# Who scales x by the gates: from GpSimd to VectorE and ScalarE, in an attention block with a mixture of experts behind it

## The chip, the cores and the metric

The kernel runs on one core of a Trainium2 chip. The metric is the device time of one execution in microseconds (us), the median of the runs: 721.62 us for the kernel before (three runs, 719.6 to 724.65). A profile of one execution, which took 726.15 us, tells what each engine did. TensorE appears in it as PE (its matmuls) and PEld (its weight loads), VectorE as DVE, ScalarE as ACT, GpSimd as POOL, SyncE as SP; a q behind the name means the engine's sequencer. SP, ACT and POOL can issue DMAs.

## The reference

Two blocks, one behind the other. First causal attention with a sliding window of 64, over 8 batches, 8 heads, 576 positions and a head dimension of 64:

```python
scores = scale * np.matmul(q, k.transpose(0, 1, 3, 2))
mask = (rel >= 0) & (rel < window)          # rel: query position minus key position
attn = softmax(np.where(mask, scores, -1e9))
attn_out = np.matmul(attn, v)
```

Its result, with the heads side by side, is x: 4608 tokens of 512 values. Then a mixture of 8 experts. Each token goes to one expert, and its result is scaled by that expert's share:

```python
logits = x @ w_gate                         # [4608, 8]
expert_idx = argmax(logits); gate_w = softmax(logits)[expert_idx]
h = np.maximum(x_sorted[lo:hi] @ w1[e], 0.0)   # tokens sorted by expert; w1: 512 x 1024
y_sorted[lo:hi] = h @ w2[e]                     # w2: 1024 x 512
out = gate_w[:, None] * y                       # back in the order of the tokens
```

Since the gate is positive, scaling x by it before the expert gives the same result as scaling y behind it. That is what the kernel does.

## The kernel before

**The attention phase** takes the first 218 us or so of the profile. The batches are worked in four *pairs* (`bg` 0 to 3) of two batches. A pair is 9 token tiles of 128 tokens (`NTB`), in three *chunks* of three tiles. A *unit* is a pair and two heads; there are 16 units, and each has three *steps*, one chunk each: 48 steps, `s` = 0 to 47, 12 to a pair. `step(s)` is a pipeline written out by hand, and every engine takes its instructions in the program's order:

- PE makes the scores of chunk s+1 (L628), multiplies the weights of chunk s-1 with v (`weighted`, L674), adds the logits of s-3, transposes the softmax of s (L659), transposes q and k of s+3 (L587, L595), and transposes x of s-2 (L699).
- VectorE masks the scores of s+1 and takes their row maxima (L641), copies one half of the transposed softmax of s out of PSUM (L661), divides s-1 by its row sums and writes it into x (`divided`, L684 to L688), and then does whatever is listed for the step in `todo`.
- ScalarE does the exponentials (L651), the other half's copy (L661) and the copies of the transposes (L600, L702), then its part of `todo`.
- GpSimd copies parts of v so that they lie where a matmul can read them (`load_v`, L567 to L573, issued in each third step, for the unit after next), then its part of `todo`.

`weighted` writes one PSUM bank, `banks[6]`; so its matmuls in step s+1 wait until `divided` in step s has read that bank.

x of a chunk is gathered over a pair's four units in an SBUF tile `xs` of 128 x 3 x 512. The pool has 7 buffers, taken in turn (chunk `3*bg + c`).

**Routing.** In the step behind a pair's last logits, `after` lists what remains of that pair in `todo`, counted in steps n from there (for the pairs 0 to 2, n = 0 is step 15, 27 and 39):

- `choose`: the argmax, the softmax, the gates and each token's rank at its expert, in five parts, all small operations on VectorE.
- `place` (L800): two VectorE operations on 128 x 128 bf16 for a token tile, which feed the table of slots.
- `weigh` (L807): scales one token tile of x (128 x 512, fp32) in place by its gates, one value per partition.
- `store` (L815): writes a chunk of x to DRAM (`x_dram`), as DMAs on the queue of GpSimd. A chunk that spans both batches takes two or three DMAs.

For the first two pairs, `place`, `weigh` and `store` are listed side by side; for the third pair they are packed into n = 2 to 5. Then `first_tiles` (n = 6) makes a first table of slots, for which PE waits (L907 to L914), and gathers the first expert's tokens from `x_dram` on GpSimd's queue. The fourth pair is weighed by ScalarE alone, after the attention phase.

**The expert phase** takes the rest: tiles of 256 tokens, gathered from `x_dram`, multiplied with one expert's w1 and w2, and scattered into the output. Sums of weight blocks (L140) are made on GpSimd. If an expert has more tiles than the unrolled code foresees, `any_number` runs instead; with these inputs it does not.

Of the kernel before, what the change touches and what calls it, by code (L numbers as in the profile page):

```python
# [11 lines left out]
F32 = mybir.dt.float32  # L12
# [3 lines left out]
ALU = mybir.AluOpType  # L16
AX = mybir.AxisListType
# [7 lines left out]
def _ins(ap: bass.AP, axis: int, n: int) -> bass.AP:  # L25

    dims = [list(d) for d in ap.ap]
    dims.insert(axis, [0, n])
    return bass.AP(tensor=ap.tensor, offset=ap.offset, ap=dims)


def _inner(ap: bass.AP, n: int) -> bass.AP:
    return _ins(ap, len(ap.ap), n)
# [3 lines left out]
def kernel(  # L37
# [10 lines left out]
    nc = tc.nc  # L48
    P = nc.NUM_PARTITIONS
    B, H, S, D = q.shape  # L50
    NT, DM = out.shape
    E = moe_w_gate.shape[1]
# [9 lines left out]
    NTB = BG * S // P  # L62
# [5 lines left out]
    NTILE = (NT + TB - 1) // TB + E - 1 + NE  # L68
# [27 lines left out]
    expert_i = consts.tile([P, NTILE], I32, name="expert_i")  # L96
# [4 lines left out]
    V, G = nc.vector, nc.gpsimd  # L101
# [48 lines left out]
    def sums_w1(e):  # L150
        form(left_sums(G, s1s[e % NW], *w1q(e)))

    def sums_w2(e):
        form(right_sums(G, s2s[e % NW], *w2q(e)))

    def load_w1(e):
        return nc.sync.dma_start(out=w1s[e % NW][:], in_=w1v[e])

    def load_w2(e):
        nc.sync.dma_start(out=w2s[e % NW][:], in_=w2v[e])  # L160
# [7 lines left out]
    lane = consts.tile([P, P], BF16, name="lane")  # L168
# [9 lines left out]
    with tc.tile_pool(name="tmp", bufs=1) as tmp:  # L178
# [8 lines left out]
        for i in range(BG):  # L187
# [12 lines left out]
            out=before[:], in_=ones[:], pattern=[[1, P]], compare_op=ALU.is_gt, fill=0.0, base=0,  # L200
# [6 lines left out]
    nt, cum, start, chunk0 = (consts.tile([P, E], F32, name=n) for n in ("nt", "cum", "start", "chunk0"))  # L207
    rt = ctx.enter_context(tc.tile_pool(name="rt", bufs=1))
# [26 lines left out]
    ST = 3  # L235
# [4 lines left out]
    v_m = Memory(consts.tile([P, 3 * 2 * BG * NV * 2 * VW], F32, name="v_m"))  # L240
# [27 lines left out]
    def form_all(parts):  # L268
        for _ in parts:
            pass  # L270

    def gather(tokens):
        G.tensor_copy(out=at_g[:], in_=tokens)
        for c in range(C):
            G.indirect_dma_start(  # L275
                out=xg[c], out_offset=None, in_=x_dram[:, :],
                in_offset=bass.IndirectOffsetOnAxis(ap=at_g[:, c : c + 1], axis=0),
            )
# [31 lines left out]
    def turned_blocks():  # L310

        rows = xg_all.rearrange("p c (g b j) -> p c g b j", b=P // QD, j=QD)
        for a in range(P // QD):
            for b in range(P // QD):
                V.transpose(  # L315
                    out=xn[b * QD : (b + 1) * QD, :, :, a * QD : (a + 1) * QD].rearrange("p c g i -> p (c g) i"),
                    in_=rows[a * QD : (a + 1) * QD, :, :, b, :].rearrange("p c g j -> p (c g) j"),
                )
                yield
# [5 lines left out]
    def keep_turned():  # L325
        for c in range(C):
            nc.scalar.copy(out=xq[:, :, c], in_=xn[:, c])  # L327
# [151 lines left out]
    def body(e, last, after, full, between=None, next_x=True):  # L479

        finish()
        scatter(perm_i[:, last])
        if between is not None:
            between()
        blocks = turned_blocks() if next_x else iter(())
        if not full:
            half_tile(e, blocks, after, next_x)
            return
        form_all(hidden(e, blocks))
        parts = output(e, blocks, next_x)  # L490
        next(parts)
        if after is not None:
            gather(perm_i[:, after])
        form_all(parts)

    with tc.manual_schedule(), ExitStack() as held, ExitStack() as brief:
# [381 lines left out]
        def after(s, routing, bg):  # L878

            do = lambda n, op: todo.setdefault(s + n, []).append(op)  # L880
            part = lambda: next(routing, None)
            if bg < last - 1:
                for n in range(5):
                    do(n, part)

                for m in range(NTB):
                    do(5 + m * 2 // 3, partial(place, bg * NTB + m))
                    do(5 + m * 2 // 3, partial(weigh, bg, m, G))
                    if m % ST == ST - 1:
                        do(5 + m * 2 // 3, partial(store, bg, m // ST, G))  # L890
                return

            for n in (0, 0, 1, 2, 2):
                do(n, part)
            for m in range(NTB):
                do(3 + m // 3, partial(place, bg * NTB + m))
                do((2, 2, 3, 3, 4, 4, 4, 5, 5)[m], partial(weigh, bg, m, nc.scalar if m in (2, 6) else G))
                if m % ST == ST - 1:
                    do(3 + m // ST, partial(store, bg, m // ST, G))
            do(6, first_tiles)  # L900
# [153 lines left out]
    with tc.manual_schedule():  # L1054
        load_w1(1)
        load_w2(1)
        def at(n):
            n = nc.s_assert_within(
                n, 0, NTILE - 1, skip_runtime_bounds_check_because="a tile with a token is one of the NTILE"
            )  # L1060
            return lambda ahead: bass.ds((n + ahead) * C, C)

        def expert(e):

            fulls, tiles, first = regs[e]
            if 0 < e < E - 1:
                load_w1(e + 1)
                load_w2(e + 1)

            def one(n, full, between=None):  # L1070
                slots = at(first + n)
                ends = e == E - 1 and (n == KT - 1 or not full)
                body(e, slots(0), None if ends or e == E - 1 and n == KT - 2 else slots(3), full, between, not ends)

            def more(n, between=None):

                with tc.If(tiles > n) as some_left:  # L1077
                    with tc.If(fulls > n, preferred_fallthrough_block=False) as full:
                        one(n, True, between)
                        if n + 1 < KT:  # L1080
                            more(n + 1)
                    with full.Else():
                        one(n, False, between)
                if between is not None:
                    with some_left.Else():
                        between()

            if e:
                one(0, True, partial(sums_w2, e))
            more(1 if e else NE, partial(sums_w1, e + 1) if e + 1 < E else None)  # L1090

        def any_number():

            tiles_of = rt.tile([P, E, NTILE], F32, name="tiles_of")
            V.tensor_tensor(
                out=tiles_of[:], in0=_inner(cum[:], NTILE), in1=_ins(lane[:, 0:NTILE], 1, E), op=ALU.is_le
            )
            with nc.allow_low_precision("integers"):
                V.tensor_reduce(out=expert_i[:], in_=tiles_of[:].rearrange("p e t -> p t e"), axis=AX.X, op=ALU.add)
            _, (tiles,) = nc.values_load_multi_w_load_instructions(  # L1100
                places_i[0:1, E : E + 1], min_val=0, max_val=NTILE,
                skip_runtime_bounds_check_because="a sum of numbers of tiles, at most NTILE for any tokens",
            )
            with tc.For_i(NE, tiles) as i:
                _, (e,) = nc.values_load_multi_w_load_instructions(
                    expert_i[0:1, bass.ds(i, 1)], engines=(mybir.EngineType.SP,), min_val=0, max_val=E - 1,
                    skip_runtime_bounds_check_because="a tile that is numbered belongs to an expert",
                )
                for w, view in ((w1s[0], w1v), (w2s[0], w2v)):
                    nc.sync.dma_start(out=w[:], in_=view[bass.ds(e, 1)].rearrange("o p n d -> (o p) n d"))  # L1110
                sums_w1(0)
                sums_w2(0)
                slots = at(i)
                gather(perm_i[:, slots(1)])
                form_all(turned_blocks())
                keep_turned()
                sums_x([xn[:, c] for c in range(C)])
                form_all(hidden(0))
                form_all(output(0, iter(()), False))
                finish()  # L1120
                scatter(perm_i[:, slots(1)])

        with tc.If(most < KT + 1) as few:  # L1123
            for e in range(E):
                expert(e)
            finish()
            scatter(perm_i[:, bass.ds(end * C, C)])
        with few.Else():
            finish()
            scatter(perm_i[:, NE * C : (NE + 1) * C])  # L1130
            any_number()
# [28 lines left out]
```

## Time and profile before

| what | us |
|---|---|
| median of the runs (lowest, highest) | 721.62 (719.6, 724.65) |
| the profiled execution, its span | 726.15, 724.4 |
| PE / VectorE / ScalarE / GpSimd busy | 689.7 / 497.8 / 258.5 / 350.7 |
| `weigh` on GpSimd (L813) | 25 x 1.565 = 39.2 |
| `weigh` on ScalarE (L811) | 11 x 0.71 = 7.3, two of them in the third pair |
| `place` on VectorE (L802) | 72 operations, 29.2 |
| `load_v`'s copies on GpSimd (L567, L569, L573) | 45.6 |
| start of VectorE's mask in step 19, 20, 21 | 97.39, 102.56, 106.45 |
| in step 27, 28, 29 | 129.34, 133.94, 137.68 |
| in step 31, 32, 33 | 145.47, 150.04, 154.13 |
| in step 39, 40, 41 | 176.69, 182.13, 185.90 |
| in step 42, 43, 44, 45 | 191.74, 195.70, 200.73, 205.49 |

The page gives the busy time of each engine, its 40 slices, and the costliest groups of instructions by line. The busy share is a mean over phases with different limits, so the steps around the change are read by themselves. A step is told here by the start of VectorE's first mask (L641) in it, which is its first instruction of that step. "Start to start" is the time from the start of one instruction to that of the next on an engine that does not idle; on VectorE it is shorter than the duration shown, since two instructions overlap at their ends.

### The profile page before, as it was taken

How to read it: one execution, taken by the hardware profiler on the slowest of the kernel's cores; microseconds unless marked ns; L12 is line 12 of the kernel's file. 1: busy time of each engine (PE TensorE's matmuls, PEld its weight loads, DVE VectorE, ACT ScalarE, POOL GpSimd, SP SyncE). 2: the span in 40 equal slices, each digit the busy share in tenths (PEclk: the TensorE clock that was granted, in tenths of full speed). 3: DMA queues.
4: the chain of work that ended last, by engine and by line, in shares of the span. 5: the costliest groups of instructions: out<-in, count | busy, mean ns of one | idle time of the engine just before them, and what ended most of it. 6: DMA issues, size and time to landing. Idle time of an engine off the chain costs nothing. (4 is left out here: it accounts for less than half of the span.)

```text
span 724.4 us, 17946 instructions
## 1 busy us (share of the span) xinstructions
PE 689.7 (95%) x6882; PEld 607.1 (84%) x6882; DVE 497.8 (69%) x1636; ACT 258.5 (36%) x653; POOL 350.7 (48%) x360
## 2 busy tenths in 40 slices
PE   5999999999879999999999999999999999999993
PEld 3887788888768898797999999899889799889993
DVE  3575898898965858675866686677766677666731
ACT  4787788888754211111211221112111111111110
POOL 4213748459375025937462356445274745272011
PEclk9999999999999999999999999999999999999997
DMA  8998898789361382715211531440261620111000
GB/s 159 219 195 186 176 188 230 168 188 235 106 194 47 121 291 81 258 59 202 102 38 60 161 133 57 154 170 30 88 243 59 242 69 30 61 37 61 2 30 28
DMA packets 137289, 93.37 MB, mean 129 GB/s; under 512 B 117009, under 2 KB 117009, under 8 KB 137171
## 3 DMA queue, kind: packets, MB, share of 16 engines
q1 hardware_dynamic: 127858, 62.16, 32.5%
q0 software_dynamic: 8736, 27.53, 11.7%
q10 hardware_dynamic: 576, 2.10, 0.9%
q8 instruction: 74, 1.21, 0.7%
q14 instruction: 45, 0.36, 0.2%
HBM read 72.89 MB, written 20.45 MB: 129 GB/s over the span
## 5 line engine op out<-in xcount | busy, mean ns | idle before, releaser
L315 DVE STREAM_TRANSPOSE v_m<-qk_m 32x256 f32<-32x256 f32 x304 | 132.4, 435 | 9.0 <-DMA qk_m<-x_dram,at_g 3.4
L344 PE MATMUL bank<-qk_m,s 128*128 128x128 f32 x1024 | 122.5, 275 | 1.0 <-DVE qk_m L365 1.0
L344 PEld LDWEIGHTS bank<-qk_m,s 128*128 128x128 f32 x1024 | 118.3, 192 | 1.2 <-issue 1.2
L275 POOL DMA_INDIRECT qk_m<-x_dram,at_g x38 | 41.0, 1080 | 142.4 <-DVE v_m L315 114.0
L651 ACT ACTIVATE pr<-pr,mx 128x128 f32<-128x128 f32 x288 | 89.7, 391 | 36.3 <-DVE mx L641 36.3
L344 PE MATMUL bank<-qk_m,w 128*128 128x128 f32 x768 | 93.8, 275 | 1.0 <-PEq L1077 0.9
L344 PEld LDWEIGHTS bank<-qk_m,w 128*128 128x128 f32 x768 | 90.6, 192 | 4.6 <-issue 4.2
L641 DVE CUSTOM_DVE_ANT_0 pr<-bank,mask 128x128 f32<-128x128 f32 x288 | 64.4, 286 | 30.7 <-PE bank L628 28.1
L295 POOL DMA_INDIRECT out_dram<-v_m,at_s x42 | 42.5, 1012 | 87.7 <-DVE v_m L384 85.1
L384 DVE TENSOR_TENSOR v_m<-bank,v_m 128x256 f32<-128x256 f32 (+1 forms) x95 | 43.8, 480 | 45.0 <-PE bank L388 30.1
L569 POOL COPY v_m<-v_m 64x520 f32<-64x520 f32 x32 | 19.8, 619 | 73.1 <-DMA v_m<-in_v_dram 72.5
L140 POOL TENSOR_TENSOR s<-w 128x1024 f32<-128x1024 f32 x22 | 52.2, 2372 | 0.0
L674 PEld LDWEIGHTS bank<-v_m,pT 128*64 128x64 f32 x1152 | 41.3, 141 | 12.0 <-DVE xs L688 5.8
L674 PE MATMUL bank<-v_m,pT 128*64 128x65 f32 x1152 | 47.9, 232 | 2.9 <-DVE xs L688 2.8
L388 PE MATMUL bank<-qkT_m,v_m 128*128 128x256 f32 x216 | 48.3, 379 | 0.0
L351 ACT COPY qk_m<-bank 128x512 f32<-128x512 f32 x16 | 9.4, 587 | 108.8 <-PE bank L344 63.2
L628 PE MATMUL bank<-qkT_m 64*64 64x128 f32 x1152 | 45.9, 290 | 0.1
L388 PEld LDWEIGHTS bank<-qkT_m,v_m 128*128 128x128 f32 x216 | 41.0, 190 | 5.5
L595 PE MATMUL bank<-ident,qk_m 128*128 128x128 f32 x256 | 37.0, 288 | 8.9 <-DMA qk_m<-in_q_dram 7.7
L444 PEld LDWEIGHTS bank<-qk_m,w 128*128 128x128 f32 x320 | 43.9, 190 | 0.9 <-issue 0.7
L444 PE MATMUL bank<-qk_m,w 128*128 128x160 f32 x320 | 44.4, 299 | 0.4 <-ACT qk_m L327 0.4
L659 PE MATMUL bank<-ident,pr 128*128 128x128 f32 x288 | 43.1, 287 | 0.0
(174 smaller groups left out, 1231.1 us busy)
## 6 DMA issues: line engine op xcount, KB each, us to landing
w<-in_moe_w_dram SPq DMA_DIRECT2D x11, 2048.0 KB, 10.0
qk_m<-in_q_dram SPq DMA_DIRECT2D x72, 128.0 KB, 3.8
qk_m<-in_k_dram SPq DMA_DIRECT2D x72, 128.0 KB, 3.7
v_m<-in_v_dram SPq DMA_DIRECT2D x64, 128.0 KB, 3.9
qk_m<-in_moe_w_dram SPq DMA_DIRECT2D x3, 2048.0 KB, 10.4
x_dram<-xs POOLq DMA_DIRECT2D x6, 512.0 KB
x_dram<-xs POOLq DMA_DIRECT2D x3, 768.0 KB
w<-in_moe_w_dram ACTq DMA_DIRECT2D x4, 512.0 KB, 4.3
```

The lines of the kernel that those rows point to most:

```text
L140: op()
L295: put = G.indirect_dma_start(out=out[:, :], out_offset=bass.IndirectOffsetOnAxis(ap=at_s[:, c : c + 1], axis=0), in_=ys[c], in_offset=None ...
L315: V.transpose(out=xn[b * QD : (b + 1) * QD, :, :, a * QD : (a + 1) * QD].rearrange("p c g i -> p (c g) i"), in_=rows[a * QD : (a + 1) * QD ...
L344: nc.tensor.matmul(acc[:, f, :], lhsT=a[:, g, f * P : (f + 1) * P], rhs=b[:, g, :], start=(first and f == 0 and g == 0), stop=(g == HG - 1 ...
L384: plus = lambda out, a, b: V.tensor_tensor(out=out, in0=a, in1=b, op=ALU.add)
L388: nc.tensor.matmul(acc, lhsT=a[:, f, :], rhs=b[:, f, :], start=(start and f == 0), stop=(stop and f == HF - 1), skip_group_check=True,)
L444: nc.tensor.matmul(acc[:, i], lhsT=w1[:, g, f * P : (f + 1) * P], rhs=xq[:, g].rearrange("p c s -> p (c s)")[:, 0:HALF], start=(i + g == 0 ...
L628: nc.tensor.matmul(out_, lhsT=qT[rows, t, a * WINDOW : (a + 1) * WINDOW], rhs=rhs, start=True, stop=True, skip_group_check=True,)
L641: V.tensor_tensor_reduce(out=prs[h][:, m, :], in0=scs[h][:, m, :], in1=mask[:, m0 + m, :], scale=-scale, scalar=-2 * MASKED, op0=ALU.add, ...
L651: nc.scalar.activation(out=y, in_=y, func=AF.Exp, scale=-1.0, bias=mx[:, h, m : m + 1])
L659: nc.tensor.transpose(out=tr[:, m, :], in_=prs[h][:, m, :], identity=ident[:])
L674: nc.tensor.matmul(px[a * D : (a + 1) * D, h, m, :], lhsT=pTs[h][:, m, a * D : (a + 1) * D], rhs=vt[:, h, :], start=True, stop=True, skip_ ...
```

## The change

`weigh` of the first two pairs goes from GpSimd to VectorE, one token tile a step in n = 4 to 12, and `place` is spread in the same way, one tile a step in n = 5 to 13. Before, both stood at n = 5 to 10, in steps of two, one, two, one tiles. The stores stay on GpSimd's queue, each in the step of its chunk's last `weigh`: n = 6, 9 and 12 instead of 6, 8 and 10.

In the third pair the seven `weigh` that GpSimd had are shared out: ScalarE has tiles 0, 1, 3 and 6 (before: 2 and 6), VectorE the other five. They stand at n = 2, 3, 3, 4, 4, 4, 5, 5, 5 instead of 2, 2, 3, 3, 4, 4, 4, 5, 5. Its `place` and `store` stay where they were.

In `any_number`, which is not run here, a table no longer has an SBUF tile of its own but lies in memory that the expert phase uses.

```diff
                 for m in range(NTB):
-                    do(5 + m * 2 // 3, partial(place, bg * NTB + m))
-                    do(5 + m * 2 // 3, partial(weigh, bg, m, G))
+                    do(5 + m, partial(place, bg * NTB + m))
+                    do(4 + m, partial(weigh, bg, m, V))
                     if m % ST == ST - 1:
-                        do(5 + m * 2 // 3, partial(store, bg, m // ST, G))
+                        do(4 + m, partial(store, bg, m // ST, G))
                 return
...
                 do(3 + m // 3, partial(place, bg * NTB + m))
-                do((2, 2, 3, 3, 4, 4, 4, 5, 5)[m], partial(weigh, bg, m, nc.scalar if m in (2, 6) else G))
+                do((2, 3, 3, 4, 4, 4, 5, 5, 5)[m], partial(weigh, bg, m, nc.scalar if m in (0, 1, 3, 6) else V))
                 if m % ST == ST - 1:
                     do(3 + m // ST, partial(store, bg, m // ST, G))
...
-            tiles_of = rt.tile([P, E, NTILE], F32, name="tiles_of")
+            tiles_of = v_m(2080, E, NTILE)
             V.tensor_tensor(
-                out=tiles_of[:], in0=_inner(cum[:], NTILE), in1=_ins(lane[:, 0:NTILE], 1, E), op=ALU.is_le
+                out=tiles_of, in0=_inner(cum[:], NTILE), in1=_ins(lane[:, 0:NTILE], 1, E), op=ALU.is_le
             )
```

More of the change, by code (lines that the diff above doesn't have):

```diff
@@ L1092, in any_number @@
         def any_number():
-            tiles_of = rt.tile([P, E, NTILE], F32, name="tiles_of")
+            tiles_of = v_m(2080, E, NTILE)
             V.tensor_tensor(
-                out=tiles_of[:], in0=_inner(cum[:], NTILE), in1=_ins(lane[:, 0:NTILE], 1, E), op=ALU.is_le
+                out=tiles_of, in0=_inner(cum[:], NTILE), in1=_ins(lane[:, 0:NTILE], 1, E), op=ALU.is_le
             )
             with nc.allow_low_precision("integers"):
-                V.tensor_reduce(out=expert_i[:], in_=tiles_of[:].rearrange("p e t -> p t e"), axis=AX.X, op=ALU.add)
+                V.tensor_reduce(out=expert_i[:], in_=tiles_of.rearrange("p e t -> p t e"), axis=AX.X, op=ALU.add)
             _, (tiles,) = nc.values_load_multi_w_load_instructions(
```

## The prediction, made before the result was known

> **What bounds the kernel now.** I read the page's busy times first, then its 40 slices, then a table of windows (us from the start; busy time of each engine, then the granted clock, DMA share, GB/s), then who waits, then the VectorE, PE and GpSimd timelines.
>
> ```profile
> PE 689.7 (95%) x6882; PEld 607.1 (84%) x6882; DVE 497.8 (69%) x1636; ACT 258.5 (36%) x653; POOL 350.7 (48%) x360
> ...
> POOL 4213748459375025937462356445274745272011
> ```
> ```profile
> 102.50:129.30 26.80, 26.19 (x453) 21.68 (x455) 24.11 (x133) 23.17 (x70) 23.37 (x27) 1.00 0.83 205
> 150.00:173.00 23.00, 22.68 (x397) 18.75 (x393) 21.48 (x116) 20.02 (x60) 19.38 (x27) 1.00 0.91 225
> 173.00:191.70 18.70, 18.17 (x321) 15.17 (x318) 15.68 (x87) 13.61 (x42) 12.46 (x14) 1.00 0.58 159
> 191.70:205.50 13.80, 11.78 (x205) 9.41 (x204) 13.60 (x68) 11.14 (x31) 8.56 (x8) 1.00 0.53 179
> ```
>
> PE is busy for 95% of the span. In the first two windows, where GpSimd weighs the first and the second pair, PE is full (26.19 of 26.80, 22.68 of 23.00) and VectorE is close behind (24.11, 21.48). In the fourth, the third pair's, it is the other way round: VectorE has 13.60 of 13.80 and PE 11.78. GpSimd is not the bound in any. What it weighs, only its own stores wait for:
>
> ```profile
> L813 POOL TENSOR_SCALAR xs<-xs,gate x25: 1554/1565/1632, 103.9 to 205.3; 128x512 f32<-128x512 f32 x25
> ...
> who waited for it (us, times):
>   POOL x_dram L822: 8.7, 3
>   POOL x_dram L829: 0.9, 3
> ```
>
> So 25 x 1.565 = 39.2 us of GpSimd go, and by themselves are worth nothing. The change is paid or repaid on VectorE. PE waits for it in two ways: weighted (L674) for the division L688, which frees its one bank, and once for L907:
>
> ```profile
> PE bank L914 <- DVE hi_e L907: 2.7, 1, 2.7
> PE bank L674 <- DVE xs L688: 2.6, 4, 0.9
> ```
>
> GpSimd does cost VectorE something. The same three pairs of L802, first with GpSimd idle, then beside L813:
>
> ```profile
> 195.26 0.31 DVE L802 TENSOR_SCALAR lo<-lane,low,tok_a 128x128 bf16<-128x128 bf16 x1
> 195.48 0.31 DVE L802 TENSOR_SCALAR lo<-lane,low,tok_b 128x128 bf16<-128x128 bf16 x1
> ```
> ```profile
> 199.16 0.30 DVE L802 TENSOR_SCALAR lo<-lane,low,tok_a 128x128 bf16<-128x128 bf16 x1
> 199.39 0.74 DVE L802 TENSOR_SCALAR lo<-lane,low,tok_b 128x128 bf16<-128x128 bf16 x1
> 199.99 0.30 DVE L802 TENSOR_SCALAR lo<-lane,low,tok_a 128x128 bf16<-128x128 bf16 x1
> ```
>
> Idle, a place (two L802) takes 0.44 from start to start; beside L813, 0.83. That is what the change can win.
>
> **The price of one weigh on VectorE, w.** No row has this operation on VectorE. TENSOR_TENSOR from SBUF takes 0.421 for 256 elements and 0.689 for 512: 0.153 fixed and 1.05 ns per element written, while reading two. If one input of 512 goes by elements read, it is 0.153 + 0.27 = 0.42; if by elements written, 0.69 (L452, TENSOR_SCALAR of 480 from PSUM, has 0.657). Both ends are equally near, so I take the middle, 0.55. Start to start is 0.09 less than a duration (L802: 0.31 against 0.22): w = 0.46, ends 0.33 and 0.60. The Trainium skill, "VectorE: DVE Perf Modes", section on the perf-mode tier table, has fp32 tensor_scalar in SBUF at two elements a cycle (1227 ns for 2048); my estimate from it is 0.42 for 512, which is the low end, and the sum would be +1.3 by it instead of +2.6.
>
> A rule against the change: the Trainium skill, "GPSIMD Engine Reference", section 4.1 Engine selection, calls one-input elementwise work on GpSimd "roughly line-rate", so moving it would win nothing. L813's 1.565 us, 3.06 ns an element, disagrees; the sum does not use it.
>
> **Step by step.** A step of VectorE is mask, copy L661, division: 2.69 us when nothing is waited for (118.15 to 120.84), 3.3 when the copy waits for PE's transposes, then the listed ops. PE's own step is 3.42, 3.96 or 4.18 (steps 4 to 8, with nothing listed on VectorE), 3.83 on average. So the listed ops may take 3.83 - 2.69 = 1.14 before VectorE becomes the bound.
>
> *Steps 21-26 and 33-38* (0.9 in each: a place and a weigh): 2.69 + 0.90 = 3.59 a step, under 3.83. After a short PE step VectorE comes 3.3 + 0.9 - 3.42 = 0.8 late; in steps 21 and 33 it is 1.6 and 1.45 late now and PE has no gap there. Cost 0, hidden behind PE; without that cover, 0.9 a step less the collisions that go.
>
> *Steps 19 and 31* get one weigh each after the routing arithmetic, where VectorE is late already: in the steps behind, L674 starts 0.05 after L688 ended and PE has a gap (0.48 at 104.83, 0.1 at 152.7). A later L688 goes straight through: 0.46 twice. Steps 20 and 32 place one tile instead of two, so the lateness does not pass on. **+0.92** (0.66 to 1.20).
>
> *Steps 27 and 28* get a place and a weigh, and a place, beside the next routing. VectorE's step 28 starts at 134.83 instead of 133.94, 1.4 behind PE's scores; step 29 starts 0.8 late, and 0.8 cost 0.1 in step 32. **+0.3** (0 to 0.9).
>
> *Steps 39 and 40*, the same for the second pair, hit the third pair's routing, which VectorE already bounds (step 39 is 5.45 long, PE waits for L661 at 183.72). Step 39 starts 0.72 late, gets back 0.56 since L661 no longer waits, and has 0.90 more: 183.19 instead of 182.13. The place in step 40 goes into 0.4 idle. **+1.0** (0.9 to 1.2).
>
> *Steps 42-45.* VectorE is never idle from 191.74 to L907 at 208.3, so all counts. Five weighs: 5 x 0.46 = 2.30. Without L813 the six L802 take 1.33 instead of 2.40 (198.33 to 200.73) in step 43 and 2.14 (203.35 to 205.49) in step 44: -1.88. **+0.42** (-0.23 to +1.12). ScalarE's four weighs (0.707 each, two more than now) fall in steps 41 to 44, where it waits for the mask; cost 0, at most 0.7 if that wait went.
>
> *Stores.* GpSimd's queue holds v's copies (L567-L573) too. The store of chunk 1 moves from step 23 to 24 (35 to 36), behind the copies of the v load issued there, which wait for its DMA. That load's last issue ends at 118.78, lands 3.9 later (the page's median), its copies end by 124, the store is issued by 125 (now 121.3), and lands 3.2 to 6.2 later: 131 at worst. Its buffer, one of seven, is written again by L688 in step 27 at 132.07: cost 0, with about 1 us left, and the like in step 39 (179.4). Chunk 2 goes from step 25 to 27, behind copies that wait till 140.4; its buffer is wanted only in step 37. The third pair's last store now lands at 211.7, and the gather behind it waits for perm_e from VectorE until 212.75: a free GpSimd brings nothing there. The moved table tiles_of lies in a branch that is not run: 0.
>
> **Sum**: 0.92 + 0.3 + 1.0 + 0.42 = **+2.6 us** (1.3 to 4.4). After 211 PE is full (497 of 513), so it stays to the end. The profiled execution took 726.15 (span 724.4): 728.8 for it. The runs' median is 721.62, 4.5 below that execution; the same difference gives **724.2**, 0.4% slower. About 1% is what a measurement of this kernel can tell from no change.
>
> **Rivals.**
> 1. *Slower: VectorE becomes the bound in every weighing step.* If a weigh costs the high end and collides with v's copies as L802 does (0.60 + 0.4 = 1.0), the listed ops are 1.44: over 1.14, the point from which it decides (w above 0.70). Steps 21-26 and 33-38 then cost 12 x 0.30 = 3.6, steps 19 and 31 2.0, 27-28 1.4, 39-40 1.5, 42-45 5.0 - 1.88 = 3.1: +11.6, 733. For: L796 took 0.60 instead of 0.17 beside a copy at 101.1. Against: copies fill only 2.9 of some 11.5 us. 0.09.
> 2. *The store of chunk 1 lands late* and L688 waits for it: some 1.5 us twice on top of the forecast, 727. For: the thin margin. Against: the worst landing was assumed. 0.10.
> 3. *Slightly faster.* The low w, and VectorE's added lateness lies under waits that PE has anyway: steps 42-45 give -0.23, the rest nothing, and copies done earlier spare 1 to 2 us of collisions: 720. PE's gaps between 90 and 211 that VectorE causes are 0.48 + 0.29 + 0.24 + 1.42 + 0.48 + 2.71 = 5.6 us; even all of them are 0.8%, which speaks against more. 0.20.
> 4. *The change does not do what it says*: L813 stays in the profile. Nothing points to it. 0.01, 721.6.
>
> **Chances.** Forecast 0.60. Faster by over 1%: 0.04 (only past all of those gaps). Slower by over 1%: rival 1, and a little of 2: 0.11. Within: 0.85. The range takes in rivals 2 and 3 and the spread of the runs (719.6 to 724.65): 718.5 to 729.
>
> **What would show it.** POOL's 39 us at L813 are gone; VectorE has 23 TENSOR_SCALAR xs<-xs,gate of 0.42 to 0.69; L802 is back at 0.31 in steps 43 and 44; no weighing step of 21-26 has a new PE gap; the gap ahead of L914 stays near 2.7 and comes some 2.6 us later than 205.9. Wrong I would be if w is over 0.70, if L688 waits for x_dram, or if PE's gaps shrink.

## The result, and the profile after

The changed kernel takes 724.39 us (median of 13 runs, 723.03 to 728.24) beside 722.33 for the kernel before (13 runs, 719.6 to 724.69). The ratio is 1.0036, with a 95% interval of 1.0020 to 1.0052: 0.4% slower, within what was called no change, but a real loss. The ratio makes it 2.6 us (1.4 to 3.8); the two medians are 2.1 apart. The forecast was 724.2 and +2.6. The size was right; of the terms that made it up, only some were.

From the page of the changed kernel: its span, busy times, instructions and GpSimd's slices (lines left out are marked by dots):

```profile
span 722.7 us, 17947 instructions
...
PE 688.7 (95%) x6882; PEld 606.5 (84%) x6882; DVE 500.7 (69%) x1659; ACT 259.9 (36%) x655; POOL 311.1 (43%) x335
...
POOL 5223734234155025947462356545275745272011
```

GpSimd lost 39.6 us of work. VectorE gained only 2.9, although its 23 weighs add 11.6. Most of the difference came back from its places (L802), which went from 29.2 to 22.7 us, now that GpSimd stretches them less. The weigh and the place on VectorE, by line (durations in ns: least, median, greatest):

```profile
L813 DVE TENSOR_SCALAR xs<-xs,gate x23: 471/479/719, 97.8 to 204.1; 128x512 f32<-128x512 f32 x23
```
```profile
L802 DVE TENSOR_SCALAR lo<-lane,low,tok_a x36: 303/306/632, 100.8 to 251.3; 128x128 bf16<-128x128 bf16 x36
L802 DVE TENSOR_SCALAR lo<-lane,low,tok_b x36: 301/307/659, 101.0 to 251.6; 128x128 bf16<-128x128 bf16 x36
```

A weigh takes 0.479 us, 0.396 from start to start (0.55 and 0.46 were taken, within 0.42 to 0.69). The greatest duration of a place's operation fell from 0.958 to 0.659.

The single profile of the kernel before began its step 19 at 97.39, 3.5 us later than that of the changed kernel (93.91), for reasons that lie ahead of any weighing. So that span (724.4) stands above the span after (722.7), and only stretches behind step 19 can be compared. A second profile of each kernel was taken for that (the runs *before_again* and *after_again* below), with step 19 at 94.30 and 94.37. (All fourteen profiles of this document have it between 93.1 and 98.7.) Each row is a stretch of steps, from the start of VectorE's first mask in the first to that in the step behind the last, in us:

| steps | before, twice | changed, twice | forecast of the difference |
|---|---|---|---|
| 19, 20 | 9.06, 8.10 | 8.11, 8.19 | +0.46 |
| 21-25 | 19.33, 19.33 | 19.19, 18.99 | 0 |
| 26-28 | 11.90, 11.90 | 14.40, 14.23 | +0.3 |
| 29, 30 | 7.79, 7.83 | 7.62, 7.71 | 0 |
| 31, 32 | 8.66, 8.75 | 8.76, 8.58 | +0.46 |
| 33-37 | 18.99, 18.99 | 19.37, 19.20 | 0 |
| 38-41 | 18.62, 18.62 | 19.34, 19.81 | +1.0 |
| 42-44 | 13.74, 13.74 | 13.85, 13.85 | +0.42 |
| 19-44 | 108.10, 107.27 | 110.64, 110.55 | +2.6 |

The whole is +2.5 to +3.4. From step 45 to the end the two kernels are alike: 518.9 and 519.3 us before, 518.1 and 519.3 changed. How far such a stretch varies by itself shows in steps 19 and 20, where five of the profiles ran the schedule of before (7.41 to 9.06 us) and four the changed one (7.81 to 8.40).

The largest part, +2.4 in steps 26 to 28, is where the forecast had 0.3. What happens there is one wait, and PE idles with it. Steps 27 and 28 in the changed kernel, then in the second profile of the kernel before (stretch, its length, busy times of PE, PEld, VectorE, ScalarE and GpSimd, granted clock, DMA share, GB/s):

```profile
125.48:135.60 10.12, 8.14 (x132) 6.46 (x128) 7.84 (x46) 6.59 (x19) 0.29 (x1) 1.00 1.24 208
```
```profile
125.30:133.63 8.33, 8.33 (x146) 7.01 (x148) 6.93 (x39) 6.92 (x20) 5.71 (x7) 1.00 0.81 203
```

VectorE's timeline of the changed kernel in step 27 (start, duration, engine, line, operation; in brackets the idle time before it and who ended it):

```profile
127.21 0.15 DVE L684 TENSOR_SCALAR rec<-bank 128x6 f32<-128x6 f32 x1
127.39 0.19 DVE L685 RECIPROCAL rec<-rec 128x6 f32<-128x6 f32 x1
129.63 0.56 DVE L688 TENSOR_TENSOR xs<-bank,rec 128x384 f32<-128x384 f32 x1 [2.04 <-DMA x_dram<-xs]
130.10 0.31 DVE L802 TENSOR_SCALAR lo<-lane,low,tok_a 128x128 bf16<-128x128 bf16 x1
```

L688 wants to write the next pair's x into the buffer of the first pair's chunk 1, and the store of that chunk has not landed. GpSimd's timeline tells why the store was late:

```profile
114.07 0.29 POOL L567 COPY v_m<-qk_m 64x128 f32<-64x128 f32 x1
121.21 0.62 POOL L569 COPY v_m<-v_m 64x520 f32<-64x520 f32 x1 [6.85 <-DMA v_m<-in_v_dram]
...
123.48 0.51 POOL L573 COPY v_m<-v_m 64x390 f32<-64x390 f32 x1
123.93 1.30 POOL L822 DMA_DIRECT2D x_dram<-xs  x2
```

GpSimd idles for 6.85 us in the copies of a v load, with the store behind them in its queue. The last of its two DMAs is issued by 125.23, and L688 is let go at 129.63. In the second profile of the kernel before, which began step 19 as early, the same store stands ahead of those copies and goes out at 119.54, 4.4 us sooner; L688 in step 27 does not wait:

```profile
119.54 1.36 POOL L822 DMA_DIRECT2D x_dram<-xs  x2
120.94 0.32 POOL L567 COPY v_m<-qk_m 64x128 f32<-64x128 f32 x1
121.30 0.62 POOL L569 COPY v_m<-v_m 64x520 f32<-64x520 f32 x1
```

What PE waited for in the attention phase after the change (total us, times, longest):

```profile
PE bank L674 <- DVE xs L688: 3.5, 6, 1.0
PE bank L699 <- DVE pT L661: 3.2, 3, 1.4
PE bank L914 <- DVE hi_e L907: 2.7, 1, 2.7
```

The waits for L688 grew from 2.6 us in the first profile of the kernel before to 3.5, and the wait for L907 stayed at 2.7, as forecast.

### The profile page after: what moved, and what is told of

The parts are those of the page before. It is cut to its first block, busy times and chain, and to the rows that moved or that the text cites. A ratio compares the mean times of both kernels' runs of the same rounds, so it can differ in the third digit from the quotient of the medians.

```text
span 722.7 us, 17947 instructions
## 1 busy us (share of the span) xinstructions
PE 688.7 (95%) x6882; PEld 606.5 (84%) x6882; DVE 500.7 (69%) x1659; ACT 259.9 (36%) x655; POOL 311.1 (43%) x335
```

## The experiments

Two theories stood against each other. **Theory 1**, the forecast's: VectorE pays for what was added in steps where it is late already. **Theory 2**: the late store. The runs' medians are spread by several us, so an interval on a ratio is some 0.2 to 0.3% to each side; the stretches from the profiles are finer, but each is from one execution, and varies by itself as said above.

**The store ahead of the v load again** (e1_store_ahead). Tile 5 is weighed one step earlier, all else as changed:

```diff
-                    do(4 + m, partial(weigh, bg, m, V))
+                    do((4, 5, 6, 7, 8, 8, 10, 11, 12)[m], partial(weigh, bg, m, V))
                     if m % ST == ST - 1:
-                        do(4 + m, partial(store, bg, m // ST, G))
+                        do((4, 5, 6, 7, 8, 8, 10, 11, 12)[m], partial(store, bg, m // ST, G))
```

> The changed kernel, but tile 5 of the first two pairs is weighed one step earlier, so that the store of chunk 1 stands in step 23 (35) as in the kernel before, ahead of the copies of the v load of step 24 (36). Theory 1 (the price: VectorE's added operations meet steps where it is late already): nothing changes, some 724.4, +2.0 us on the kernel before. Theory 2 (the late store: the division L688 in step 27 waits 2.0 us for the store of chunk 1, whose buffer it writes again): the wait is gone, 722.3 to 722.8, within 0.5 us of the kernel before, and steps 27 and 28 take some 8.4 instead of 10.1 us.

Measured: 724.97 us, ratio 1.0027 (1.0001 to 1.0054). L688 waited for no DMA; steps 27 and 28 took 8.13 us instead of 10.12, and steps 19 to 44 108.87 instead of 110.64 and 110.55. So in the profile the late store was worth 1.7 of the 2.5 to 3.4 us. The medians don't show that gain: 1.7 us off the changed kernel's 1.0036 would make 1.0013, and the interval of e1 holds that and no gain as well. How much of the measured loss the wait makes up over many executions is not shown. Steps 38 to 41 took 19.80, no less than in the changed kernel: that part of theory 1 stands by itself.

**Only the stores late** (e2_late_stores). The kernel before, weighing on GpSimd, with the stores' new steps:

```diff
-                        do(5 + m * 2 // 3, partial(store, bg, m // ST, G))
+                        do(4 + m, partial(store, bg, m // ST, G))
```

> The kernel before, with GpSimd weighing as it did, but the stores of the first two pairs listed where the changed kernel has them (n = 6, 9, 12). Theory 1: VectorE has nothing new, so no difference, 0 us. Theory 2: L688 waits for x_dram in step 27, perhaps also in step 39, for 1 to 2 us each: +1 to +3 us.

Measured: 724.21 us, ratio 1.0016 (0.9990 to 1.0042). The time alone can't tell it from no change. In the profile the wait is there, without one weigh on VectorE; steps 27 and 28 took 9.80 instead of 8.33. VectorE's line of L688 in this kernel's timeline:

```profile
130.24 0.56 DVE L688 TENSOR_TENSOR xs<-bank,rec 128x384 f32<-128x384 f32 x1 [2.15 <-DMA x_dram<-xs]
```

Here the copies ahead of the store did not wait for their DMA (they ran from 119.35 to 122.50); their own length was enough, and the store went out at 122.44. With e1 this settles that the wait comes with the store's place in GpSimd's queue, not with the engine that weighs. It came in step 27 alone; step 39, for which the same was feared, never waited in any profile.

**Each half of the change by itself** (e3_first_two_pairs, e4_third_pair). In e3 the third pair's line of `weigh` is as before; in e4 the three lines of the first two pairs are.

> The change in the first two pairs alone; the third pair as before, with GpSimd weighing seven tiles. From the prediction's terms with the measured 0.40 us a weigh: steps 19 and 31 0.8, 27 and 28 0.3, 39 and 40 0.95: +2.0 us on the kernel before. Theory 2 gives +2 for another reason. If the relief in the third pair is worth more than I worked out, this kernel is slower than the changed one, +3 or more.

> The change in the third pair alone; the first two pairs as before, on GpSimd. The prediction's term for steps 42 to 45 with the measured 0.40 us a weigh: 5 x 0.40 - 1.88 = +0.1 us. A rival, that the collisions of VectorE with GpSimd cost more than those seen in L802: -1 us or less.

Measured: the first two pairs alone 725.45 us, ratio 1.0039 (1.0014 to 1.0064), with L688 waiting 3.17 us; the third pair alone 722.12 us, 0.9996 (0.9971 to 1.0022). No loss is shown outside the first two pairs. Steps 42 to 44, in which VectorE is the bound, took 13.86 us with the third pair's change and 13.77 without it: five weighs on VectorE cost 5 x 0.40 = 2.0 and the end of the collisions gave 1.9 back, as worked out. In e4 L688 waited 1.30 us too, with the old steps of the stores: there three weighs of GpSimd stand ahead of the store, which went out at 122.07 instead of 119.54. The first two pairs of e4 are those of the kernel before, so that kernel is at the edge of this wait itself.

**Nothing weighed in the first two pairs** (e5_no_weigh). The changed kernel with this line taken out; tokens of those pairs go into the experts unscaled:

```diff
-                    do(4 + m, partial(weigh, bg, m, V))
```

> The changed kernel without the weighing of the first two pairs (their tokens go unscaled into the experts); places, stores and the third pair as changed. So the price of the 18 weighs on VectorE is measured by itself. Theory 1 (they are paid in steps 19, 31 and 39, 0.40 us each, and nowhere else): 1.2 us less from step 19 to step 46 than in the changed kernel, and the wait of L688 for x_dram, if that comes with the store's place, stays. Theory 2 (all of the loss is the late store): no less than 116.5 us from step 19 to step 46 (changed kernel 116.9), and L688 waits about 2 us.

Measured: 724.13 us, ratio 1.0028 (1.0009 to 1.0047), still slower than the kernel before, with no weigh at all in the first two pairs. L688 waited 1.78 us for x_dram. Steps 19 to 44 took 108.23, 2.4 less than the changed kernel. Most of it lies in steps 19 and 20 (6.95 against 8.11) and 31 and 32 (7.92 against 8.76), and none in steps 21 to 25 and 33 to 37 (19.60 and 19.60, against 19.19 and 19.37). So the weighs in those ten steps are free, and the others look paid for, by one execution.

**Each weigh twice** (e6_twice), to look for the point from which VectorE decides:

```diff
                 engine.tensor_scalar(out=y, in0=y, scalar1=s, scalar2=None, op0=ALU.mult)
+                if bg < last - 1:
+                    engine.tensor_scalar(out=y, in0=y, scalar1=1.0, scalar2=None, op0=ALU.mult)
```

> The changed kernel with each weigh of the first two pairs done twice on VectorE (the second time by 1.0, same tile): some 0.38 us more in each of the 18 steps. The prediction's threshold says that the listed operations of a step cost nothing up to 1.14 us; here they are 0.44 + 0.40 + 0.38 = 1.22, so 12 x 0.08 = 1.0 us in steps 21 to 26 and 33 to 38, and 0.38 each in steps 19, 27, 31 and 39: +2.5 us on the changed kernel. If VectorE is the bound in all of those steps already, 18 x 0.38 = +6.8. If PE hides it all, 0.

Measured: 731.7 us, ratio 1.0112 (1.0092 to 1.0132): by the two ratios 0.76% or some 5.5 us above the changed kernel, twice what was expected, and most of the 18 x 0.34 = 6.1 us that were added. (Its profile began step 19 at 98.73, and L688 of step 27 came only at 130.86 and did not wait, though the store stood where the changed kernel has it.) Busy times in steps 21 to 25 and 33 to 37, first in the changed kernel, then in this one (stretch, its length, PE, PEld, VectorE, ScalarE, GpSimd, granted clock, DMA share, GB/s):

```profile
102.02:121.20 19.18, 19.15 (x329) 15.88 (x325) 17.79 (x97) 17.05 (x51) 5.91 (x12) 1.00 0.92 209
151.98:171.35 19.37, 19.37 (x343) 16.37 (x340) 17.89 (x97) 17.34 (x51) 7.61 (x15) 1.00 0.87 207
```
```profile
107.81:128.61 20.80, 20.00 (x337) 16.22 (x339) 20.29 (x102) 17.44 (x51) 7.91 (x15) 1.00 0.88 217
159.24:179.27 20.03, 19.75 (x337) 16.20 (x339) 19.52 (x102) 17.44 (x51) 7.95 (x15) 1.00 0.81 206
```

With one weigh a step PE fills the stretch and VectorE has 1.4 us left. With two, VectorE has 0.5 left and PE has gaps of 0.8 and 0.3: the bound is passing over, at 0.44 + 0.40 + 0.34 = 1.18 us listed a step. That agrees with a threshold of 1.14, which lies between 0.84 (free) and 1.18 (not free). The price beyond it was too low: 1.6 and 0.7 us for the two stretches against 0.4 each.

**Another packing** (e7_packed). Places and weighs of the first two pairs in steps 20 to 26 (32 to 38), clear of the routing, stores in steps 21, 23 and 26:

```diff
-                    do(5 + m, partial(place, bg * NTB + m))
-                    do(4 + m, partial(weigh, bg, m, V))
+                    do((5, 6, 7, 8, 9, 9, 10, 11, 11)[m], partial(place, bg * NTB + m))
+                    do((5, 6, 6, 7, 8, 8, 9, 10, 11)[m], partial(weigh, bg, m, V))
                     if m % ST == ST - 1:
-                        do(4 + m, partial(store, bg, m // ST, G))
+                        do((5, 6, 6, 7, 8, 8, 9, 10, 11)[m], partial(store, bg, m // ST, G))
```

> The changed kernel with weighs and places of the first two pairs packed into steps 20 to 26 (32 to 38): none meets the routing in steps 19, 27, 28, 31, 39 and 40, and the stores of chunks 1 and 2 stand in steps 23 and 26, ahead of the next v load. Listed operations a step: 0.84 to 1.28 us. Theory 1: the 0.95 of steps 39 and 40 and the 0.8 of 19 and 31 go, 0.5 comes in the fuller steps. Theory 2: the wait of L688 goes. Both together: within 0.5 us of the kernel before, 722 to 723.2; 38 to 42 takes 18.3 to 18.7 us (changed kernel 19.34) and no wait of L688 for x_dram.

Measured: 724.42 us, ratio 1.0021 (1.0003 to 1.0039). No wait of L688. Steps 38 to 41 took 19.04, less than the changed kernel but above the 18.3 to 18.7 expected: step 38 now has 1.28 listed. Still slower than the kernel before, by the medians: its steps 19 to 44 took 108.30 us, where that kernel's two profiles have 107.27 and 108.10.

**The steps of before, on VectorE** (e8_steps_of_before): places, weighs and stores at `5 + m * 2 // 3`, weighed by V.

> VectorE weighs the first two pairs in the very steps in which GpSimd did it before (places and stores as before, too); third pair as changed. This parts the engine from the move. Steps 20, 22 and 24 (32, 34, 36) then hold two places and two weighs, 1.68 us, the others 0.84, 1.26 on average against the 1.14 that PE hides: 12 x 0.12 = 1.4 us by theory 1, and none of the 0.95 in steps 39 and 40: +1.4 on the kernel before. Theory 2: the store of chunk 1 is earlier than with GpSimd's weighing, so no wait of L688.

Measured: 726.03 us, ratio 1.0037 (1.0022 to 1.0053). No wait of L688, and 18.60 for steps 38 to 41, as before. But steps 21 to 25 took 20.35 and 33 to 37 19.96, 2.0 us together more than before (19.33, 18.99), where 1.4 was expected for these and steps 20 and 32. Two places and two weighs in a step are too much even if the next step has room: its steps 20 to 25 took 4.59, 3.46, 4.65, 3.46, 5.01 and 3.77 us.

**A second profile of each kernel, and two variants.** before_again is the kernel before:

> The kernel before once more, for a second profile. In the first one the steps up to 19 took 97.4 us and L688 in step 27 did not wait; in the four other profiles with the old stores or the late ones and an early start (93.6 to 95.1) it waited 1.3 to 3.2 us. If the wait hangs on how early the attention is, since the loads of v end at about the same time in every execution: with step 19 starting near 94, L688 waits about 1 us here too; with a start near 97, not.

Measured: 722.97 us, ratio 0.9985 (0.9958 to 1.0012). Step 19 began at 94.30 and L688 did not wait: the expectation was wrong. Of the five profiles with the stores in their old steps (both of the kernel before, e4, e8, e9), e4 alone shows the wait.

after_again is the changed kernel:

> The changed kernel once more, beside the other kernels of this call. With step 19 starting near 94: L688 waits 2 us, and 116.5 to 117 us from step 19 to 46. With a start near 97: no wait, and some 115. Time: 1.002 to 1.005 of the kernel before.

Measured: 726.16 us, ratio 1.0038 (1.0016 to 1.0060), the first result once more. L688 waited 2.04 us, to the hundredth as in the first profile.

e10_places_of_before puts the places back (`do(5 + m * 2 // 3, ...)`) and leaves weighs and stores as changed:

> The changed kernel with the places of the first two pairs back in their old steps (20 to 25, 32 to 37); weighs and stores as changed. Theory 1: the place leaves steps 39 and 40 (27 and 28), so steps 38 to 41 take 0.4 to 0.8 us less than the changed kernel's 19.3; steps 20, 22, 24 have 1.28 listed, 0.1 above what PE hides. Theory 2: the wait of L688 in step 27 stays, 2 us with an early start. 0.3 to 0.8 us less than the changed kernel in all.

Measured: 725.48 us, ratio 1.0032 (1.0009 to 1.0055). L688 waited 2.10 us. Steps 38 to 41 took 18.65, which is the 18.62 of before: with the places of steps 38 to 40 gone, the weighs of steps 38 and 39 alone cost nothing there. But with the places and no weighs (e5) they took 19.03, also less than the changed kernel's 19.34 and 19.81: it takes both to make the +0.7 to +1.2. Steps 19 and 20 took 8.83 instead of 8.11 and 21 to 25 19.88 instead of 19.19, so most of it was lost again, if these single executions hold.

e9_mixed leaves the first two pairs on GpSimd, but for tile 5, and has the third pair as changed:

```diff
-                    do(5 + m * 2 // 3, partial(weigh, bg, m, G))
+                    do(5 + m * 2 // 3, partial(weigh, bg, m, V if m == 5 else G))
```

> Third pair as changed; the first two pairs as before, on GpSimd, but for tile 5, which VectorE weighs in step 23 (35), so that the store of chunk 1 has one weigh of 1.57 us less ahead of it on GpSimd. Listed operations in step 23: 0.84, under 1.14, so free by theory 1; the wait of L688 (1.3 us with the first two pairs as before and an early start) goes by theory 2: 0.997 to 1.000 of the kernel before, and 113 us or less from step 19 to 46 without the throttle's part. If neither holds, 1.000 or above.

Measured: 722.63 us, ratio 0.9992 (0.9963 to 1.0021). No wait of L688, and 107.32 us for steps 19 to 44, which is no less than the better profile of the kernel before (107.27). It can't be told from the kernel before, and nothing that was run is shown to beat it.

## Why the prediction was right, and where it was wrong

**GpSimd's 39.2 us are worth nothing by themselves: right, as far as the runs show.** They went, and the kernel became slower. The third pair alone, which takes seven weighs off GpSimd, changed nothing that can be measured.

**The price of a weigh: mis-sized a little.** 0.396 start to start was measured against 0.46, nearer to the low end. By it the forecast's sum would have been some +2.1. The rule in the Trainium skill, "VectorE: DVE Perf Modes", the section on the perf-mode tier table, from which 0.42 was estimated for the duration, came closer to the measured 0.479 than the middle of the rows (0.55) did. The words "roughly line-rate" in the Trainium skill, "GPSIMD Engine Reference", section 4.1 Engine selection, against which L813's row stood, do not hold here: the same tile takes 1.565 us on GpSimd and 0.479 on VectorE. (The same row of that table names VectorE as the engine for elementwise work, and that agrees.)

**Steps 21-26 and 33-38 cost 0: right for steps 21-25 and 33-37.** They took nearly the same with GpSimd's weighs (19.33 and 18.99), with VectorE's (18.99 to 19.37), and with none (19.60). Step 26 took 0.7 us more in the first profile and 0.5 in the second; with the late store gone (e1), steps 26 to 28 together took 11.99 against 11.90. Step 38 took 0.3 and 0.5 more, which the table has in steps 38 to 41. The threshold of 1.14 is bracketed by e6, not found; the price beyond it was too low. The step that fails there is "PE's own step is ..., 3.83 on average". (The starts of VectorE's steps 4 to 8 give 3.79, and 2.69 runs to the end of L688, 0.08 past the start of the next instruction; the two slips nearly cancel.) Comparing means lets a light step pay for a heavy one. e8 speaks against that: by means its ten steps should have lost 10 x 0.12 = 1.2 us, by the four heavy ones alone (1.68 listed) 4 x 0.54 = 2.2, and they lost 2.0.

**Steps 19 and 31, +0.92: wrong.** They and the steps behind them took 8.11 and 8.19 (before: 9.06 and 8.10), and 8.76 and 8.58 (before: 8.66 and 8.75): no loss that stands out of the spread. A weigh there is not free, since leaving out the two of each stretch saved 1.2 and 0.8 in one execution (e5). What the forecast left out is a credit: it took the place that leaves steps 20 and 32 only as a reason why the lateness is not passed on, and put no price on it, nor on the places that GpSimd's weighs no longer stretch there. That these make up the difference is likely, not shown; e10, which puts the place back, took 8.83 in steps 19 and 20.

**Steps 27 and 28, +0.3: right without the wait** (e1: +0.1 in steps 26 to 28), and **the stores, "cost 0, with about 1 us left": wrong.** This is the step that failed most: +1.8 us in steps 27 and 28. The mechanism was named, as rival 2, with 0.10 and 1.5 us twice; it came once, with 2.0. The forecast of the store itself held: issued by 125.23 (125 was said), landed by 129.63 (131 at worst). What it had wrong is when the buffer is wanted. The margin was worked out from the first profile, in which L688 of step 27 stood at 132.07 because step 19 had begun at 97.39. In the changed kernel L688 was ready at 127.59 and 127.76, in the second profile of the kernel before it ran at 128.03. The v load was not earlier by as much. Its issues, in the first profile of the kernel before and of the changed kernel:

```profile
114.21 4.57 SPq L566 DMA_DIRECT2D v_m<-in_v_dram  x4
```
```profile
114.12 3.88 SPq L566 DMA_DIRECT2D v_m<-in_v_dram  x4
```

They begin at 113.54 and 113.96 in the two other profiles. The work that had to wait was 4 us and more earlier and the DMA less than 1, so a margin of 1 us, taken from one execution, was none. Why the load keeps its time was not looked into, and how many executions begin late enough to be spared is not known (e6 was one).

**Steps 39 and 40, +1.0: right in size** (+0.7 and +1.2 for steps 38 to 41), and in the mechanism: more work on VectorE in the steps of the third pair's routing, which it bounds. The shares were not what was worked out: step 39 was charged for its weigh and its place alike, but the weigh alone costs nothing (e10: 18.65).

**Steps 42-45, +0.42: right in kind.** +0.11 in steps 42 to 44, and with the measured price the same working gives 5 x 0.40 - 1.88 = +0.12.

**The sum was right by luck.** By the means of the two profiles of each kernel, steps 26 to 28 cost 2.1 us more than the forecast had, most of it a wait that was costed at nothing; steps 19, 20, 31 and 32 cost 1.4 less, and the third pair 0.3 less. What is left nearly cancels.

## What to carry to other kernels

Taking work off an engine that nobody waits for gains nothing; look first at who pays for it, and compare step by step with the longer of the two engines, not with means. When a store or any other instruction is moved in a queue that is worked in order, look at what it now stands behind, and at who writes its buffer next; a spare of 1 us in one profile is no cover. Compare profiles only behind a point up to which the kernels are the same.

## What the runs showed that I had not expected

The collision between VectorE and GpSimd also falls on the weigh itself. In the first profile of the changed kernel three weighs took 0.59 to 0.72 us instead of 0.479, each while GpSimd issued a store's DMA (L822); in the second, two took 0.85 and 0.74 beside copies of v. Other weighs beside a copy or an issue kept 0.47 to 0.48, and once it was the copy that took longer (L573 0.75 instead of 0.51). In these two profiles a weigh lost up to 0.37 us in this way, nearly the 0.39 that a place loses beside a weigh on GpSimd, so work moved to VectorE takes some of the collision along.

Step 45's length is 5.61 us in the first profile of the kernel before and 6.27 in the changed kernel, though VectorE does the same work in it (3.15 and 3.19 us busy). The granted clock tells it: the stretch, its length, the busy times, and the clock at the third place from the end, first before, then after.

```profile
205.50:211.10 5.60, 2.90 (x84) 2.42 (x84) 3.15 (x21) 2.60 (x8) 3.86 (x5) 0.97 0.53 171
```
```profile
204.60:210.90 6.30, 3.61 (x86) 3.09 (x86) 3.19 (x21) 2.60 (x8) 2.84 (x5) 0.73 0.43 137
```

The second profile of the kernel before has 0.74 and 6.30 there, and e10, with the changed third pair, 0.97 and 5.57, so the change is not its cause; it is one reason why step 45 was left out of the sums above.
